# Transposing x and the queries as fp16 pairs read as fp32, with the two head pairs of the query exponentials interleaved

## The chip, the core and the metric

The kernel runs on one core of a Trainium2 chip. The metric is the time of one execution in microseconds (us) on the device; the time of a kernel is the median over its runs. The profile of one execution gives, for every instruction, its engine, its start and its duration. The engines are PE (TensorE, matrix multiplications and transposes; its weight loads are listed apart as PEld), DVE (VectorE), ACT (ScalarE), POOL (GpSimd) and SP (SyncE, which here only issues DMAs).

## What is computed

The input q, k and v have the shape (8 batches, 8 heads, 576 rows, 64 columns). The first part is a linear attention, the second a highway layer on its output, seen as 4608 tokens of 512 columns:

```python
q_s = softmax(q, axis=-1)          # over the 64 columns of a row
k_s = softmax(k, axis=2)           # over the 576 rows of a head
kv = einsum('bhsd,bhse->bhde', k_s, v)
x = einsum('bhsd,bhde->bhse', q_s, kv)   # then (B, S, H*D) -> 4608 x 512
H = maximum(x @ w_h, 0)
T = 1 / (1 + exp(-(x @ w_t + b_t)))
out = T * H + (1 - T) * x
```

All inputs and the output are float32. The softmax of the reference subtracts the maximum first; the kernel takes the exponentials directly and divides by their sums later.

## The kernel before

**Tiles.** The eight batches are taken in pairs. Each pair gives nine tiles of 128 tokens: four from the one batch, four from the other, and one with the 64 last rows of each (`tiles`, lines 125 to 129), so 36 tiles, numbered 0 to 35.

**Steps and their order.** The work is cut into small steps, each a function that records the instructions of one step on one engine. The string `ORDER` (lines 16 to 62), written out in full, names all steps in one sequence. `eq_3_0:F` is the step `eq` with the numbers 3 and 0 and the variant F; a letter A, D or P mostly chooses the engine (ACT, DVE, POOL). Every engine does its steps strictly in the order of this string, and waits where a step needs a result or a free buffer. All loads and nearly all stores are issued by SP, whose queue is in the same order; so a load behind a store waits until that store is ready.

**Per batch b.** `k`, `v` and `q` load float32 tiles with three buffers each. `ek` (L253) takes the exponentials of k on ACT to fp16. `vc` (L259) copies v to fp16. `kv` (L269) multiplies them on PE with 64x64 tiles, `kr` and `kn` (L281, L287) divide by the sums on DVE and write the result `kvb`, block-diagonal over a pair of heads. `eq` takes the exponentials of q on ACT to fp16 (L298, L302, L307). The tile `qe` is then [128 partitions, 9 row groups j, 4 head groups c, 64 columns]; partitions hold two halves of the heads or of the rows, by the batch. `qt` transposes it on PE in pieces of 128x128 fp16 (L319, L324), `qc` (L333) copies the transposed queries from PSUM to the SBUF tile `eq`. Batch 7 is different: its main part is transposed by two DMAs (`qd`, L340), and only its last 64 rows on PE. `WIDE` are batches 4 to 7, whose q is loaded in another layout, `TURNED` is batch 7. The batches 0 and 1 take `eq` in three groups of row groups (`GROUPS`), batch 2 in two halves of head groups, batch 3 and 4 at once (F), the later ones in two halves and a remainder.

**Per tile i.** `xu` (L361) multiplies the transposed queries with `kvb` on PE and gives the unnormalised x with the sums. `rs` and `x` (L370, L376) divide on DVE and write x as fp16. `xt` (L384) transposes x on PE: four transposes of 128x128, each taking every second column of 256 (the rows of w_h and w_t are loaded in the same order, partition p of a block holding rows 2p and 2p+1). They go to the first half of the one PSUM tile `turned`. `xe` (L391) copies it to SBUF as `xT`, on DVE or ACT. `mt` (L411) and `mh` (L419) multiply xT with w_t and w_h, four multiplications of 512 columns each. `bw` (L399) writes the bias into the PSUM tile of the gate first. `th` takes a tanh (L433, L435), `dd` (L439) forms the maximum, `uu` multiplies gate and difference on DVE (L453) or, for 17 tiles, on POOL in two steps (L450, L451), and `oo` (L471) adds x on POOL. `st` stores. Tiles 0, 4 and 5 are done in two halves by head pairs (`HALVED`).

**The start.** `fill` (L167) are dummy multiplications of zeros on PE; they stand between the first steps until about 17 us.

Two identity matrices are built on POOL at the start, `idf` in fp32 and `idh` in fp16; PE's transposes use `idh` as the moving operand and the data as the weights.

Of the kernel before, what the change touches and what calls it, by code (L numbers as in the profile page):

```python
# [8 lines left out]
FP32 = mybir.dt.float32  # L9
FP16 = mybir.dt.float16  # L10
AF = mybir.ActivationFunctionType
# [54 lines left out]
def kernel(  # L66
# [10 lines left out]
    nc = tc.nc  # L77
    B, H, S, D = q.shape
    DM = H * D
    P = 128  # L80
    NP = 64
    NJ = S // NP
# [7 lines left out]
    qep = pool("qep", 2)  # L90
    eqp = pool("eqp", 4)
    xp = pool("xp", 6)
    xtp = pool("xtp", 3)
# [10 lines left out]
    idf = consts.tile([P, P], FP32, name="idf")  # L104
    idh = consts.tile([P, P], FP16, name="idh")
    w16 = {w: consts.tile([P, KC, DM], FP16, name="w16" + w) for w in "th"}
# [8 lines left out]
    turned = ps_xt.tile([P, 2, 4, P], FP16, tag="xtps", name="turned")  # L115
    spare = turned.rearrange("p a c d -> p (a c d)").bitcast(FP32)
    T = {}

    def once(name, make):
        if name not in T:  # L120
            T[name] = make()
        return T[name]
# [10 lines left out]
    def heads(i, k):  # L133
        return (k, k + 1) if i in HALVED else (0, 2)
# [6 lines left out]
    def columns(i, h):  # L141
        return slice(PIECES[h], PIECES[h + 1]) if i == LAST else slice(0, DM)

    def gate(i, h):
        return f"tps{i}_{h}" if i == LAST else f"tps{i}"
# [28 lines left out]
    def landing(which, b):  # L174
        return once(f"{which}32{b}", lambda: ld.tile([P, 4, NJ * D], FP32, tag=which, name=f"{which}32_{b}"))
# [4 lines left out]
    def load_kv(which):  # L180
        def step(e, b, c):
            n = (2 if which == "k" else 1, 2)[b] if b < 2 else 4
            nc.sync.dma_start(landing(which, b)[:, c:c + n], rows_of(which, b)[:, c:c + n])
        return step

    WIDE = (4, 5, 6, 7)
    MAIN = 4 * 2 * 4 * D
    TURNED = (7,)

    def flat_q(b):  # L190
        return landing("q", b).rearrange("p c f -> p (c f)")
# [99 lines left out]

    GROUPS = ((0, 4), (4, 8), (8, 9))

    def eq(e, b, g):
        t = once(f"qe{b}", lambda: qep.tile([P, NJ, 4, D], FP16, tag="qe", name=f"qe_{b}"))
        if b in WIDE:
            if g == 2:
                nc.scalar.activation(t[:, 8], flat_q(b)[:, MAIN:].rearrange("p (c d) -> p c d", c=4), AF.Exp)  # L298
                return
            half = slice(0, 8) if e == "F" else slice(4 * g, 4 * g + 4)  # L300
            src = flat_q(b)[:, 0:MAIN].rearrange("p (c t d) -> p c t d", c=4, t=8)[:, :, half]
            nc.scalar.activation(t[:, half].rearrange("p t c d -> p c t d"), src, AF.Exp)  # L302
            return
        js, cs = slice(*GROUPS[g]), slice(0, 4)
        if b >= 2:
            js, cs = slice(0, NJ), slice(0, 4) if e == "F" else slice(2 * g, 2 * g + 2)
        nc.scalar.activation(t[:, js, cs].rearrange("p j c d -> p c j d"),  # L307
                             T[f"q32{b}"].rearrange("p c (j d) -> p c j d", j=NJ)[:, cs, js], AF.Exp)

    def qt(e, b, g):  # L310
        j0, j1 = GROUPS[g]
        a, s = (2, 2) if g < 2 else (1, 1)
        t = T[f"qps{b}_{g}"] = ps_q.tile([P, a, 4, s * NP], FP16, tag="qps", name=f"qps_{b}_{g}")
        if b in WIDE and g < 2:
            main = T[f"qe{b}"].rearrange("p j c d -> p (j c d)")[:, 0:MAIN]
            main = main.rearrange("p (hh j kk f) -> p j hh kk f", j=4, hh=2, kk=2)
            for jp in (2 * g, 2 * g + 1):
                for n in range(4):
                    nc.tensor.matmul(t[:, jp % 2, n], main[:, jp, n % 2, n // 2], idh,  # L319
                                     is_transpose=True, start=True, stop=True, skip_group_check=True)  # L320
            return
        for j in range(j0, j1):
            for kk in range(2):
                nc.tensor.matmul(  # L324
                    t[:, (j - j0) % 2, 2 * kk:2 * kk + 2].rearrange("p n (t s u) -> p n t s u", s=s, u=2)[:, :, :, (j - j0) // 2],
                    T[f"qe{b}"][:, j, 2 * kk:2 * kk + 2].rearrange("p c d -> p (c d)"), idh,
                    is_transpose=True, start=True, stop=True, skip_group_check=True)

    def qc(e, b, g):
        copy = nc.scalar.copy if e == "A" else nc.vector.tensor_copy  # L330
# [6 lines left out]
    def qd(e, b, g):  # L337
        t = T[f"eq{b}_{g}"] = eqp.tile([P, 2, 4, P], FP16, tag="eq", name=f"eq_{b}_{g}")
        half = MAIN // 2
        nc.sync.dma_start_transpose(t.rearrange("p a n t -> p (a n) t"),  # L340
                                    T[f"qe{b}"].rearrange("p j c d -> p (j c d)")[:, g * half:(g + 1) * half])

    def turned_q(b, jp, n):
        if b in TURNED and jp < 4:
            return T[f"eq{b}_{n % 2}"].rearrange("p a n t -> p (a n) t")[:, 2 * jp + n // 2]
        return T[f"eq{b}_{jp // 2}"][:, jp % 2, n]

    def xu(e, i, k):
        bs, jp = tiles[i]
        k0, k1 = heads(i, k)  # L350
        if i in HALVED:
            t = ps_g.tile([P, DM], FP32, tag="gps", name=f"xu_{i}_{k}").unsqueeze(1)
        else:
            t = ps_x.tile([P, 2, DM], FP32, tag="xu", name=f"xu_{i}")
        T[f"xu{i}_{k}"] = t
        for n in range(2 * k0, 2 * k1):
            kk, hh = n // 2, n % 2
            for w, b in enumerate(bs):
                rows = slice(0, P) if len(bs) == 1 else slice(64 * w, 64 * w + 64)
                dst = t[rows, kk - k0, 0:260].rearrange("p (s e) -> p s e", s=4)[:, hh:hh + 3:2]  # L360
                nc.tensor.matmul(dst, turned_q(b, jp, n), kvb[b % NKV][:, hh, kk],  # L361
                                 start=True, stop=True, skip_group_check=True)
# [15 lines left out]

    def xt(e, i, k):
        k0, k1 = heads(i, k)  # L380
        t = T[f"xtps{i}"] = turned[:, 0]
        for n in range(2 * k0, 2 * k1):
            n0 = n // 2 * 2 * P
            nc.tensor.matmul(t[:, n], T[f"x{i}"][:, n0 + n % 2:n0 + 2 * P:2], idh, is_transpose=True,  # L384
                             start=True, stop=True, skip_group_check=True)

    def xe(e, i, k):
        k0, k1 = heads(i, k)
        t = once(f"xT{i}", lambda: xtp.tile([P, 4, P], FP16, tag="xT", name=f"xT_{i}"))
        copy = nc.vector.tensor_copy if e == "D" else nc.scalar.copy  # L390
        copy(t[:, 2 * k0:2 * k1], T[f"xtps{i}"][:, 2 * k0:2 * k1])  # L391


    def bw(e, i, h=0):
# [8 lines left out]
    def parts_of(i, k):  # L403
        return range(2 * k, 2 * k + 2) if i in HALVED else range(4)

    def mt(e, i, k):
        cs = columns(i, k)
        parts = parts_of(i, k)
        first = once(f"mt{i}", lambda: k) == k and len(parts) < 4
        for n in parts:  # L410
            nc.tensor.matmul(T[gate(i, k)][:, cs], T[f"xT{i}"][:, n], w16["t"][:, n, cs], start=False,  # L411
                             stop=(n == parts[-1] and not first), skip_group_check=True)

    def mh(e, i, k):
        first = f"gps{i}" not in T
        t = once(f"gps{i}", lambda: ps_g.tile([P, DM], FP32, tag="gps", name=f"gps_{i}"))
        parts = parts_of(i, k)
        for n in parts:
            nc.tensor.matmul(t, T[f"xT{i}"][:, n], w16["h"][:, n], start=(first and n == parts[0]),  # L419
                             stop=(n == parts[-1] and not (first and len(parts) < 4)), skip_group_check=True)  # L420


# [50 lines left out]
    def st(e, i, h):  # L473
# [21 lines left out]
        setuppool=setup_pool, setupdve=setup_dve, bsplit=bsplit, fill=fill,  # L495
        k=load_kv("k"), v=load_kv("v"), q=load_q, w=load_w, b=load_b, bp=bp, bc=bc,
        wtc=wt_cast, whc=wh_cast, whd=wh_less_identity, ek=ek, vc=vc, kv=kv, kr=kr, kn=kn, eq=eq, qt=qt, qc=qc, qd=qd,
        xu=xu, rs=rs, x=x, xt=xt, xe=xe, bw=bw, mt=mt, mh=mh, th=th, dd=dd, uu=uu, oo=oo, st=st)
    with tc.manual_schedule():
        for step in ORDER.split():  # L500
            name, _, eng = step.partition(":")
# [32 lines left out]
```

## Time and profile before

| | |
|---|---|
| time, median of 3 runs | 118.87 us (118.81 to 119.09) |
| span of the profiled execution | 116.9 us (no other time of this execution is given) |
| mean granted clock of TensorE | 0.995 |
| busy: PE, PEld | 109.5 us (94%), 61.6 us (53%) |
| busy: DVE, ACT, POOL | 93.3 us (80%), 90.0 us (77%), 89.1 us (76%) |
| DMA | 40.58 MB, mean 347 GB/s |
| x transposes (L384) | 144 of 128x128 fp16 |
| query transposes (L324, L319) | 80 and 48 of 128x128 fp16 |
| multiplications with w_t, w_h (L411, L419) | 148 and 144 |

How to read the rows of the profile: a row of a group gives line, engine, operation, target and sources by the program's names, shapes, the count, then the busy time in us and the mean of one instruction in ns, then the engine's idle time in front of these and what ended it. A row of waits reads "who waited, for whom: us in total, how many times, the longest". A row of the timeline or of the chain begins with the start in us and a duration in us. Matmuls are pipelined: the duration of one contains a latency that overlaps with the next, so that the distance of starts in a series, and not the mean of one, is what an instruction costs. Shares of busy time are means over the whole run; what a change is worth is read at the stage in which it lies.

### The profile page before, as it was taken

To read this page: it belongs to the slowest core of one execution; us is meant where nothing else is said; L and a number is where in the kernel's file an instruction comes from. 1 tells how busy PE (TensorE), PEld (TensorE's weight loads), DVE (VectorE), ACT (ScalarE), POOL (GpSimd) and SP (SyncE) were. 2 spreads that over 40 slices of the span, in tenths; PEclk is the share of its full clock that TensorE was granted. 3 is DMA by queue.
4 is the path that set the end of the run, shared out by engine and by line. 5 is a ranking of instruction groups with operands and counts; after the bars stand their busy time and mean duration, and the time that the engine had idled before them with its cause. 6 is when DMAs were issued, how large, how long until landed. Compare 5 with 4: busy or idle time off the path is not lost.

```text
span 116.9 us, 3424 instructions
## 1 busy us (share of the span) xinstructions
PE 109.5 (94%) x1351; PEld 61.6 (53%) x1351; DVE 93.3 (80%) x222; ACT 90.0 (77%) x132; POOL 89.1 (76%) x99
## 2 busy tenths in 40 slices
PE   5999987999999999999999999999999999999930
PEld 2354544545665656565665547566564555554520
DVE  5642587589799979979889798988989887899870
ACT  4356461897999999989999999998597998545520
POOL 5022237208996999999999999999989699999960
PEclk9999999999999999999999999999999999999998
DMA  2999999999999999999999999999999956992875
GB/s 42 399 392 377 408 398 385 375 377 379 393 391 397 383 391 393 358 375 387 357 376 360 387 392 363 390 381 383 399 398 217 302 204 270 397 404 115 315 295 179
DMA packets 24195, 40.58 MB, mean 347 GB/s; under 512 B 5362, under 2 KB 11762, under 8 KB 24180
## 3 DMA queue, kind: packets, MB, share of 16 engines
q1 hardware_dynamic: 24032, 40.24, 96.9%
q8 instruction: 10, 0.16, 0.6%
q10 hardware_dynamic: 148, 0.14, 0.4%
q14 instruction: 5, 0.04, 0.1%
HBM read 30.41 MB, written 9.44 MB: 341 GB/s over the span
## 4 chain that ended last, share of the span: by engine, by line
PE 67%; POOL 15%; issue 6%; DVE 5%; DMA 3%; SPq 1%; POOLq 0%; DVEq 0%
PE tps L411 18%; PE gps L419 16%; PE turned L167 9%; POOL o L471 7%; PE xu L361 6%; PE turned L384 5%; PE kv L269 5%; PE qps L324 4%; POOL u L451 4%; DMA out_dram<-o 3%; POOL g L450 2%; PE qps L319 2%; POOL v L259 2%; DVE x L376 2%; PE tps L401 1%
## 5 line engine op out<-in xcount | busy, mean ns | idle before, releaser
L471 POOL TENSOR_TENSOR o<-u,x 128x512 f32<-128x512 f16 (+1 forms) x36 | 40.6, 1143 | 1.6 <-DVE u L453 0.7
L411 PE MATMUL tps<-w16t,xT 128*128 128x512 f16 (+1 forms) x148 | 37.3, 373 | 0.0
L419 PE MATMUL gps<-w16h,xT 128*128 128x512 f16 x144 | 36.8, 379 | 0.5 <-DVE xT L391 0.5
L376 DVE TENSOR_TENSOR x<-xu,rs 128x512 f16<-128x512 f32 (+1 forms) x39 | 25.2, 649 | 2.4
L259 POOL CAST v<-v 128x1152 f16<-128x1152 f32 (+1 forms) x14 | 14.0, 1010 | 14.7 <-DMA v<-in_v_dram 13.7
L439 DVE SCALAR_TENSOR_TENSOR d<-x,gps 128x512 f16<-128x512 f16 x36 | 24.5, 680 | 0.3
L451 POOL TENSOR_TENSOR u<-g,d 128x512 f16<-128x512 f16 x17 | 19.7, 1158 | 1.7 <-DVE rs L370 0.4
L253 ACT ACTIVATE ek<-k 128x576 f16<-128x576 f32 (+2 forms) x15 | 17.9, 1225 | 3.0 <-DMA k<-in_k_dram 3.0
L419 PEld LDWEIGHTS <-xT 128*128 128x128 f16 x144 | 13.0, 98 | 12.3 <-DVE xT L391 1.8
L399 ACT COPY tps<-ball 128x512 f32<-128x512 f32 x28 | 16.6, 597 | 3.5 <-DVE u L453 3.2
L411 PEld LDWEIGHTS <-xT 128*128 128x128 f16 x148 | 13.2, 98 | 10.6 <-DVE xT L391 0.4
L361 PE MATMUL xu<-kvb,eq 128*128 128x130 f16 (+1 forms) x160 | 14.8, 224 | 0.2 <-DVE kvb L287 0.2
L384 PE MATMUL turned<-idh,x 128*128 128x128 f16 x144 | 14.2, 220 | 0.5 <-DVE x L376 0.5
L391 DVE COPY xT<-turned 128x512 f16<-128x512 f16 (+1 forms) x28 | 10.9, 391 | 4.2 <-PE turned L384 3.0
L435 ACT ACTIVATE tps<-tps 128x512 f32<-128x512 f32 (+1 forms) x20 | 11.2, 559 | 3.6 <-PE tps L411 3.3
L453 DVE SCALAR_TENSOR_TENSOR u<-tps,d 128x512 f16<-128x512 f32 (+1 forms) x19 | 12.7, 671 | 1.4 <-ACT tps L435 0.6
L361 PEld LDWEIGHTS <-eq 128*128 128x128 f16 (+1 forms) x160 | 10.0, 100 | 7.3 <-DVE x L376 2.5
L167 PE MATMUL turned<-blank 128*128 128x512 f16 x40 | 12.4, 458 | 1.5 <-POOL blank L149 1.3
L384 PEld LDWEIGHTS <-x 128*128 128x128 f16 x144 | 9.8, 98 | 6.0 <-DVE x L376 2.1
L307 ACT ACTIVATE qe<-q 128x1024 f16<-128x1024 f32 (+3 forms) x9 | 9.4, 1052 | 4.1 <-DMA q<-in_q_dram 4.1
L450 POOL TENSOR_SCALAR g<-th 128x512 f16<-128x512 f16 x17 | 10.6, 621 | 0.9 <-ACT th L433 0.9
L433 ACT ACTIVATE th<-tps 128x512 f16<-128x512 f32 x17 | 10.0, 594 | 0.9 <-PE tps L411 0.9
(48 smaller groups left out, 106.8 us busy)
## 6 DMA issues: line engine op xcount, KB each, us to landing
k<-in_k_dram SPq DMA_DIRECT2D x6, 1152.0 KB, 12.2
v<-in_v_dram SPq DMA_DIRECT2D x6, 1152.0 KB, 12.0
out_dram<-o SPq DMA_DIRECT2D x23, 256.0 KB, 4.0
q<-in_q_dram SPq DMA_DIRECT2D x10, 512.0 KB, 11.5
out_dram<-o SPq DMA_DIRECT2D x6, 512.0 KB, 3.8
k<-in_k_dram SPq DMA_DIRECT2D x4, 576.0 KB, 9.3
q<-in_q_dram SPq DMA_DIRECT2D x2, 1152.0 KB, 14.2
q<-in_q_dram SPq DMA_DIRECT2D x2, 640.0 KB, 10.5
```

Source lines behind the costliest of these rows:

```text
L167: nc.tensor.matmul(spare, blank[:, 0:P], blank, start=True, stop=True, skip_group_check=True)
L253: nc.scalar.activation(t[:, :, c:c + n].rearrange("p j c d -> p c j d"), T[f"k32{b}"][:, c:c + n].rearrange("p c (j d) -> p c j d", j=NJ), ...
L259: copy(v16[b % NV][:, c:c + n, :, 0:D], T[f"v32{b}"][:, c:c + n].rearrange("p c (j d) -> p c j d", j=NJ))
L361: nc.tensor.matmul(dst, turned_q(b, jp, n), kvb[b % NKV][:, hh, kk], start=True, stop=True, skip_group_check=True)
L376: nc.vector.tensor_mul(t[:, k0:k1], sums(i, k)[:, :, :, 0:64], T[f"rs{i}_{k}"][:, 0:k1 - k0].unsqueeze(3).to_broadcast([P, k1 - k0, 4, D]))
L384: nc.tensor.matmul(t[:, n], T[f"x{i}"][:, n0 + n % 2:n0 + 2 * P:2], idh, is_transpose=True, start=True, stop=True, skip_group_check=True)
L399: nc.scalar.copy(t[:, cs], ball[:, cs])
L411: nc.tensor.matmul(T[gate(i, k)][:, cs], T[f"xT{i}"][:, n], w16["t"][:, n, cs], start=False, stop=(n == parts[-1] and not first), skip_gro ...
L419: nc.tensor.matmul(t, T[f"xT{i}"][:, n], w16["h"][:, n], start=(first and n == parts[0]), stop=(n == parts[-1] and not (first and len(part ...
L439: nc.vector.scalar_tensor_tensor(t, T[f"x{i}"], -0.5, T[f"gps{i}"], op0=ALU.mult, op1=ALU.max)
L451: nc.gpsimd.tensor_mul(t, g, T[f"d{i}"])
L471: eng.tensor_add(t[:, cs], T[f"u{i}_{h}"][:, cs], T[f"x{i}"][:, cs])
```

## The change

Two fp16 elements that lie side by side are read as one fp32 element, and transposed together. A 128x128 transpose of such pairs moves 128 fp32 columns; the result holds, for each pair, the transposed two elements side by side.

- `xt`: in place of four fp16 transposes with `idh` a tile takes two fp32 ones with `idf`. The tile `xT` has the two elements of a pair innermost; `mt` and `mh` pick one of them with a step of two (`turned_x`).
- `qt`: for a row group j in place of two fp16 transposes there is one fp32 transpose, in the batches 0 to 6, and for the remainder of batch 7. `turned_q` picks with a step of two.
- `eq`: in order that the right elements be neighbours, the two head pairs (k = 0, 1) are interleaved element by element when the exponentials are written. One instruction writes one head pair, to every second fp16 element. For batches 0 and 1 in each of the two main groups, and for batches 3 and 4 (F), there are then two instructions where there was one. Batches 2, 5 and 6 had two already: their halves are now the head pairs (5 and 6 had halves of the row groups). The remainders (g = 2) stay one instruction. Batch 7's main part is written as before and still transposed by DMA.

ORDER, all pools, loads and stores stay as they are. The core of the diff (the unchanged lines around and the DMA step's renaming are cut):

```diff
     def eq(e, b, g):
...
+        exp = lambda dst, src: nc.scalar.activation(dst, src, AF.Exp)
+        pairs = flat_qe(b).rearrange("p (j w d k) -> p k w j d", j=NJ, w=2, k=2)
+        if b in WIDE and g == 2:
+            exp(pairs[:, :, :, 8], flat_q(b)[:, MAIN:].rearrange("p (k w d) -> p k w d", k=2, w=2))
+            return
+        if b in TURNED:
...
+        ks, js = (0, 1), slice(0, 8) if b in WIDE else slice(0, NJ)
+        if b >= 2:
+            ks = (0, 1) if e == "F" else (g,)
+        else:
+            js = slice(*GROUPS[g])
...
+        if b < 2 and g == 2:
+            exp(pairs[:, :, :, 8], src[:, :, :, 8])
+            return
+        for k in ks:
+            exp(pairs[:, k, :, js], src[:, k, :, js])
 
     def qt(e, b, g):
...
+        q32 = flat_qe(b).bitcast(FP32).rearrange("p (j f) -> p j f", j=NJ)
...
+        t32 = t.rearrange("p a n t -> p (a n t)").bitcast(FP32).rearrange("p (a h t) -> p a h t", a=a, h=2)
+        turn = lambda dst, src: nc.tensor.matmul(dst, src, idf, is_transpose=True, start=True, stop=True,
+                                                 skip_group_check=True)
         if b in WIDE and g < 2:
...
             for jp in (2 * g, 2 * g + 1):
-                for n in range(4):
-                    nc.tensor.matmul(t[:, jp % 2, n], main[:, jp, n % 2, n // 2], idh,
-                                     is_transpose=True, start=True, stop=True, skip_group_check=True)
+                for hh in range(2):
+                    turn(t32[:, jp % 2, hh], q32[:, 4 * hh + jp])
             return
         for j in range(j0, j1):
-            for kk in range(2):
-                nc.tensor.matmul(
...
+            turn(t32[:, (j - j0) % 2].rearrange("p h (t s u) -> p h t s u", s=s, u=2)[:, :, :, (j - j0) // 2], q32[:, j])
 
     def turned_q(b, jp, n):
...
-        return T[f"eq{b}_{jp // 2}"][:, jp % 2, n]
+        t = T[f"eq{b}_{jp // 2}"][:, jp % 2].rearrange("p n t -> p (n t)").rearrange("p (h t k) -> p h t k", h=2, k=2)
+        return t[:, n % 2, :, n // 2]
 
     def xt(e, i, k):
         k0, k1 = heads(i, k)
-        t = T[f"xtps{i}"] = turned[:, 0]
-        for n in range(2 * k0, 2 * k1):
-            n0 = n // 2 * 2 * P
-            nc.tensor.matmul(t[:, n], T[f"x{i}"][:, n0 + n % 2:n0 + 2 * P:2], idh, is_transpose=True,
+        T[f"xtps{i}"] = turned[:, 0].rearrange("p n t -> p (n t)").rearrange("p (c t r) -> p c t r", c=2, r=2)
+        pairs, turned_pairs = T[f"x{i}"].bitcast(FP32), spare[:, 0:2 * P].rearrange("p (c t) -> p c t", c=2)
+        for c in range(k0, k1):
+            nc.tensor.matmul(turned_pairs[:, c], pairs[:, c * P:(c + 1) * P], idf, is_transpose=True,
                              start=True, stop=True, skip_group_check=True)
 
+    def turned_x(i, n):
+        return T[f"xT{i}"][:, n // 2, :, n % 2]
...
-            nc.tensor.matmul(T[gate(i, k)][:, cs], T[f"xT{i}"][:, n], w16["t"][:, n, cs], start=False,
+            nc.tensor.matmul(T[gate(i, k)][:, cs], turned_x(i, n), w16["t"][:, n, cs], start=False,
...
-            nc.tensor.matmul(t, T[f"xT{i}"][:, n], w16["h"][:, n], start=(first and n == parts[0]),
+            nc.tensor.matmul(t, turned_x(i, n), w16["h"][:, n], start=(first and n == parts[0]),
```

More of the change, by code (lines that the diff above doesn't have):

```diff
@@ L292, with flat_qe @@
     GROUPS = ((0, 4), (4, 8), (8, 9))
+    def flat_qe(b):
+        return once(f"qe{b}", lambda: qep.tile([P, NJ * 4 * D], FP16, tag="qe", name=f"qe_{b}"))
     def eq(e, b, g):
-        t = once(f"qe{b}", lambda: qep.tile([P, NJ, 4, D], FP16, tag="qe", name=f"qe_{b}"))
-        if b in WIDE:
[L297 to L302, printed above, removed]
-            return
[L304 to L308, printed above, removed]
+        exp = lambda dst, src: nc.scalar.activation(dst, src, AF.Exp)
[4 more added lines that the diff above has]
+        if b in TURNED:
+            src = flat_q(b)[:, 0:MAIN].rearrange("p (c t d) -> p t c d", c=4, t=8)[:, 4 * g:4 * g + 4]
+            exp(flat_qe(b)[:, 0:MAIN].rearrange("p (t c d) -> p t c d", t=8, c=4)[:, 4 * g:4 * g + 4], src)
+            return
[4 more added lines that the diff above has]
+            js = slice(*GROUPS[g])
+        if b in WIDE:
+            src = flat_q(b)[:, 0:MAIN].rearrange("p (k w j d) -> p k w j d", k=2, w=2, j=8)
+        else:
+            src = T[f"q32{b}"].rearrange("p (k w) (j d) -> p k w j d", k=2, j=NJ)
+        if b < 2 and g == 2:
+            exp(pairs[:, :, :, 8], src[:, :, :, 8])
+            return
+        for k in ks:
+            exp(pairs[:, k, :, js], src[:, k, :, js])
     def qt(e, b, g):
@@ L312, in qt @@
         a, s = (2, 2) if g < 2 else (1, 1)
+        q32 = flat_qe(b).bitcast(FP32).rearrange("p (j f) -> p j f", j=NJ)
         t = T[f"qps{b}_{g}"] = ps_q.tile([P, a, 4, s * NP], FP16, tag="qps", name=f"qps_{b}_{g}")
+        t32 = t.rearrange("p a n t -> p (a n t)").bitcast(FP32).rearrange("p (a h t) -> p a h t", a=a, h=2)
+        turn = lambda dst, src: nc.tensor.matmul(dst, src, idf, is_transpose=True, start=True, stop=True,
+                                                 skip_group_check=True)
         if b in WIDE and g < 2:
-            main = T[f"qe{b}"].rearrange("p j c d -> p (j c d)")[:, 0:MAIN]
-            main = main.rearrange("p (hh j kk f) -> p j hh kk f", j=4, hh=2, kk=2)
             for jp in (2 * g, 2 * g + 1):
-                for n in range(4):
-                    nc.tensor.matmul(t[:, jp % 2, n], main[:, jp, n % 2, n // 2], idh,
-                                     is_transpose=True, start=True, stop=True, skip_group_check=True)
+                for hh in range(2):
+                    turn(t32[:, jp % 2, hh], q32[:, 4 * hh + jp])
             return
         for j in range(j0, j1):
-            for kk in range(2):
[L324 to L327, printed above, removed]
+            turn(t32[:, (j - j0) % 2].rearrange("p h (t s u) -> p h t s u", s=s, u=2)[:, :, :, (j - j0) // 2], q32[:, j])
     def qc(e, b, g):
@@ L340, in qd @@
         nc.sync.dma_start_transpose(t.rearrange("p a n t -> p (a n) t"),
-                                    T[f"qe{b}"].rearrange("p j c d -> p (j c d)")[:, g * half:(g + 1) * half])
+                                    flat_qe(b)[:, g * half:(g + 1) * half])
     def turned_q(b, jp, n):
@@ L388, in xe @@
         k0, k1 = heads(i, k)
-        t = once(f"xT{i}", lambda: xtp.tile([P, 4, P], FP16, tag="xT", name=f"xT_{i}"))
+        t = once(f"xT{i}", lambda: xtp.tile([P, 2, P, 2], FP16, tag="xT", name=f"xT_{i}"))
         copy = nc.vector.tensor_copy if e == "D" else nc.scalar.copy
-        copy(t[:, 2 * k0:2 * k1], T[f"xtps{i}"][:, 2 * k0:2 * k1])
+        copy(t[:, k0:k1].rearrange("p c t r -> p (c t r)"),
+             T[f"xtps{i}"][:, k0:k1].rearrange("p c t r -> p (c t r)"))
+    def turned_x(i, n):
+        return T[f"xT{i}"][:, n // 2, :, n % 2]
     def bw(e, i, h=0):
```

## The prediction

> **What bounds the kernel now.** I read the page's strip of 40 slices first, then busy time by stretch, the chain that ended last, and the waits of POOL. The strip (tenths busy per slice of 2.9 us) shows that from slice 8 on nothing has room:
>
> ```profile
> PE   5999987999999999999999999999999999999930
> DVE  5642587589799979979889798988989887899870
> ACT  4356461897999999989999999998597998545520
> POOL 5022237208996999999999999999989699999960
> DMA  2999999999999999999999999999999956992875
> ```
>
> PE runs from slice 7 on without a hole; POOL is full from about 27 us, ACT from about 26 to 82 us, and the DMA engines from 3 to 87 us. Busy PE can be a slow PE, so the chain matters more (start, us, engine, line):
>
> ```profile
> 70.69 0.45 PE qps L319 x8
> ...
> 73.03 0.86 PE gps L419 x4
> ...
> 75.97 0.22 PE turned L384 x4
> ```
>
> Between 20 and 83 us the chain is made of PE steps that follow each other at exactly such lengths. Eight query transposes take 0.45 us, 56 ns each; four x transposes 0.22 us; four multiplications of 512 columns 0.86 us, 215 ns each. So on PE the number of moving columns sets the time. The weight loads lie under it, though one alone is longer than a transpose:
>
> ```profile
> L411 PEld LDWEIGHTS <-xT 128*128 128x128 f16 x148 | 13.2, 98 | 10.6 <-DVE xT L391 0.4
> L384 PEld LDWEIGHTS <-x 128*128 128x128 f16 x144 | 9.8, 98 | 6.0 <-DVE x L376 2.1
> ```
>
> The second row is also the answer to an edit below: L384 already loads every second fp16 column of x, at 98 ns, the same as the contiguous load of L411.
>
> From 83 us on the chain runs through POOL. POOL's work from 27 us on is a queue in fixed order, and it hardly waits (its other five groups of waits all end by 26.56 us and are left out):
>
> ```profile
> POOL v L259 <- PE tps L411: 0.9, 1, 0.9
> POOL g L450 <- ACT th L433: 0.9, 1, 0.9
> POOL o L471 <- DVE u L453: 0.7, 2, 0.5
> POOL u L451 <- DVE rs L370: 0.4, 1, 0.4
> ```
>
> ```profile
> 26.56 0.67 POOL L259 CAST v<-v 128x576 f16<-128x576 f32 x1 [3.86 <-DMA v<-in_v_dram]
> ...
> 111.61 1.82 POOL L471 TENSOR_TENSOR o<-u,x 128x512 f32<-128x512 f16 x2 [0.49 <-DVE u L453]
> ```
>
> Its stretch begins at 26.56, released by a load and not by PE, and ends at 113.43. All its waits inside add to 0.9 + 0.9 + 0.7 + 0.4 = 2.9 us. The change takes no work from POOL, so **2.9 us is the most that any saving on PE can give**.
>
> **The profiled execution.** Its span is 116.9 us; the median of the runs shown is 118.87, 1.97 more. I take those 1.97 us as outside the span and unchanged, and state times against the median.
>
> **The change on PE.** Every pair of fp16 transposes becomes one transpose of the same 128 moving columns, with elements of four bytes. Where they stand, in the stretch in which PE has no hole (us, busy and count of PE, then of the loads):
>
> ```profile
> 20.00:112.00 92.00, 13.42 (x136) 9.30 (x136) 1.00 1.01 356
> 20.00:112.00 92.00, 5.63 (x62) 3.98 (x62) 1.00 1.01 356
> 20.00:112.00 92.00, 3.67 (x48) 3.03 (x48) 1.00 1.01 356
> ```
>
> These are x (L384), and the queries (L324, L319): 246 transposes, which become 123. The 26 before 20 us lie among dummy multiplications and waits and I cost them at nothing; their cover is the fill work (L167). No fp32 matmul or load stands in this trace. The bounds: the cheapest is the row of equal column count, 56 ns, so a pair goes from 112 to 56 and PE loses 123 x 56 ns = 6.9 us. The dearest is the row of four times the columns, 215 ns (four passes): PE gains 123 x (215 - 112) = 12.7 us. Even is 112 ns. I take 56, or up to about 100 if the weight load of 98 ns shows: it is nearest in kind, the same operation with the same number of columns, and columns are what set every PE row above.
>
> The Trainium skill, "TensorE: Matmul & The Clock Gate", section Terms, says of the transpose mode that loads and multiplications got on trn2 that it makes FP32 four times faster; by that a pair costs one pass and PE saves the 6.9 us. No run so far shows it.
>
> **The other edits on PE.** The multiplications by w_t, w_h and the xu products now load every second column of xT and eq: 98 ns by the L384 row above, against 98, so nothing. The copies out of PSUM (L391, L333) move the same flat fp16 elements: nothing. DMA bytes, the queue order of SP and POOL, and batch 7's two DMA transposes are untouched.
>
> **The change on ACT.** The query exponentials are split by head pair where one instruction covered both: eq_0_0, eq_0_1, eq_1_0, eq_1_1, eq_3 and eq_4, six instructions more. The fixed cost of one, from two lengths:
>
> ```profile
> L307 ACT ACTIVATE qe<-q 128x1024 f16<-128x1024 f32 x4 | 4.2, 1058 | 4.1 <-DMA q<-in_q_dram 4.1
> L307 ACT ACTIVATE qe<-q 128x2304 f16<-128x2304 f32 x1 | 2.1, 2127 | 0.0
> L253 ACT ACTIVATE ek<-k 128x2304 f16<-128x2304 f32 x5 | 10.6, 2122 | 0.0
> L302 ACT ACTIVATE qe<-q 128x2048 f16<-128x2048 f32 x1 | 1.9, 1919 | 0.0
> ```
>
> (2127 - 1058) / 1280 = 0.835 ns per element, and 1058 - 1024 x 0.835 = 203 ns fixed: 1.2 us in all. Of the first four, three are done before PE comes to their turn; behind eq_1_0 the turn waits,
>
> ```profile
> PEld L324 <- ACT qe L307: 0.6, 1, 0.6
> ```
>
> so 0.2 us of it reach PE; eq_3 and eq_4 add 0.4 to a full ACT (41 and 53 us), of which ACT's own waits on PE take back some. I charge 0.5 us. Writing at a step of two fp16 elements is in no row; lower bound nothing (it writes the same count), upper bound double the 0.835 ns for 7 x 2304 elements, 13.5 us. I take nothing: L253 and L302, with other layouts of source and target, fit the same rate (203 + 2048 x 0.835 = 1913, measured 1919).
>
> **What of 6.9 us can reach the end.** A faster PE meets the loads. The last k tile is issued, lands (a window that holds this issue alone), is exponentiated, and then used for kv on PE:
>
> ```profile
> 77.69 0.59 SPq L183 DMA_DIRECT2D k<-in_k_dram  x1
> ```
>
> ```profile
> DMA to landing us min/median/max: 11.5/11.5/11.5
> ```
>
> ```profile
> 90.11 2.12 ACT L253 ACTIVATE ek<-k 128x2304 f16<-128x2304 f32 x1
> ```
>
> ```profile
> 92.80 0.78 PE L269 MATMUL kv<-v,ek 64*64 64x65 f16 x72
> 93.51 0.40 PE L384 MATMUL turned<-idh,x 128*128 128x128 f16 x4
> ...
> 108.88 0.39 PE L384 MATMUL turned<-idh,x 128*128 128x128 f16 x4
> ```
>
> It lands at 77.69 + 11.5 = 89.2, with the DMA engines full until 87 us by the strip; the earliest end of its exponential is 91.3, so this kv step (92.80) can move by about 1.4 us and no more, though PE has saved 107 x 56 ns = 6.0 us by then. Behind it stand seven x turns (the first and last shown) and two short q turns, 16 pairs: 16 x 56 = 0.9 us. Together 2.3 us, under POOL's 2.9. Less 0.5 for ACT: 1.8, and 0.1 for handovers that do not close up: a gain of 1.7 us, **117.2 us** (span 115.2). This hardly depends on the exact price: with each weight load after a group's first exposed, two x turns take 98 + 56 = 154 instead of 222 ns and four q turns 350 instead of 448; by 92.8 us that is 27 x 68 + 13 x 98 ns = 3.1 us, still more than 1.4, the tail gives 0.5, and the end gains about 1.3: 117.6.
>
> **Rivals.**
>
> *Four passes.* An fp32 matrix multiplication split into passes would cost 215 ns per turn, by the 512-column row. PE is full from 20 to 112 us, so 12.7 us go straight to the end, with 0.5 of ACT: 132 us. It decides from 112 ns up. Against it: nothing in the profile; for it: nothing either. The Trainium skill, "FP8 and Floating Point Precision", TensorE Precision Notes, says that true FP32 takes four passes through the array; that is a statement on products, and gives the 132 us if turns are treated alike. Chance 0.15.
>
> *The weight load no longer hides (the other side of my forecast).* Today 98 ns of load lie under 56 ns turns, so two loads overlap. If a four-byte load cannot run under the turn before it, each fp32 turn costs 98 + 56 = 154 ns, 42 more than the pair it replaces; 123 x 42 = 5.2 us, on a PE without holes: 118.87 + 5.2 + 0.5 = 124.5. It decides from 56 ns of exposed load per turn. For it: in the profile a load is longer than a turn; against: 512 columns ahead of a first turn hide a load. The Trainium skill, "TensorE: Matmul & The Clock Gate", section Weight-path perf modes, says that the fast weight load is off for FP32 input, and the section LDWEIGHTS gives columns / 1.2 ns: an estimate of 107 ns, 163 ns per turn and 125.6 us by it. Chance 0.13.
>
> *Hidden anyway.* If POOL's waits and the k_7 landing do not move at all, because loads queue behind stores that POOL paces, the saving ends as PE idle and ACT's 0.5 us cancel the 0.9 of the tail: 118.5, within 0.3% of 118.87 to slightly faster. Chance 0.08.
>
> *ACT becomes the bound.* PE saves, but strided exponentials run slower by half, 6.7 us more on an ACT that is full between 26 and 82 us and idles only 1 to 2 us in it; some 2 to 5 us reach the end: 121 to 124. It decides from about 20% more per element. Against: the single rate above. Chance 0.07.
>
> **How the numbers follow.** Forecast 0.57 (117.2, own range 116.2 to 118.3), hidden 0.08, ACT 0.07, exposed load 0.13, four passes 0.15. Below 116.2 (POOL's 2.9 us nearly all gained) I leave 0.04; the four-pass time at 132 is left out above; so 116.2 to 125.6 holds 0.81. Against the 0.3% that a measurement tells here (0.36 us): faster is the forecast but for 0.04 of it that lands short, and a little of "hidden", 0.55; same 0.07; slower 0.38, the last three rivals and some loss by the order of work.
>
> **What would show it.** Right: two fp32 turns of x per tile at about 0.11 us together in the chain, and half as many query turns; POOL waits under 2.9 us in sum; PE with holes that wait for DVE x or xT; ek of batch 7 waiting for its k load near 89 us; ACT 1.2 us busier. Wrong: two turns that take 0.3 or 0.43 us, PE full and everything else with gaps; interleaved exponentials of 1152 elements longer than 1.2 us; or POOL's first o later than 27.2 us.

## The result, and the profile after

The changed kernel takes 120.31 us (120.22 to 120.87), the kernel before, run beside it, 118.93: a ratio of 1.0131, 95% interval 1.0108 to 1.0154. It is slower by about 1.4 us (difference of the medians) to 1.6 us (by the ratio), where 117.2 us was forecast. The span of the profiled execution is 118.6 us against 116.9.

First the turns (a turn is one transpose on PE). This is PE's timeline of the changed kernel (start, duration, line, operation, count):

```profile
45.43 0.39 PE L394 MATMUL turned<-idf,x 128*128 128x128 f32 x2
45.65 0.60 PE L328 MATMUL qps<-idf,qe 128*128 128x128 f32 x4
46.09 1.03 PE L425 MATMUL tps<-w16t,xT 128*128 128x512 f16 x4
...
85.56 0.43 PE L371 MATMUL xu<-kvb,eq 128*64 128x130 f16 x8
85.92 0.44 PE L394 MATMUL turned<-idf,x 128*128 128x128 f32 x2
86.19 1.03 PE L425 MATMUL tps<-w16t,xT 128*128 128x512 f16 x4
```

From start to start, two fp32 turns take 45.65 - 45.43 = 0.22 us, four 0.44: 0.11 us each, as much as the two fp16 turns that each replaces. PE saved nothing. In the last group, behind a step with 64-wide weights, the pair takes 0.27; the same group of the kernel before takes 0.24:

```profile
84.07 0.43 PE L361 MATMUL xu<-kvb,eq 128*64 128x130 f16 x8
84.43 0.40 PE L384 MATMUL turned<-idh,x 128*128 128x128 f16 x4
84.67 1.03 PE L411 MATMUL tps<-w16t,xT 128*128 128x512 f16 x4
```

The weight loads became longer, and the interleaved exponentials too (groups by shape of the changed kernel; the last two numbers before the second bar are busy us and the mean in ns):

```profile
L394 PEld LDWEIGHTS turned<-idf,x 128*128 128x128 f32 x72 | 8.6, 141 | 5.9 <-DVE x L386 1.8 <-ACT xT L401 0.9 <-DVE xT L401 0.2
L298 ACT ACTIVATE qe<-q 128x1024 f16<-128x1024 f32 x8 | 10.3, 1300 | 0.0
L298 ACT ACTIVATE qe<-q 128x1152 f16<-128x1152 f32 x4 | 5.8, 1500 | 0.0
L298 ACT ACTIVATE qe<-q 128x512 f16<-128x512 f32 x8 | 5.6, 763 | 4.5 <-DMA q<-in_q_dram 4.5
L401 DVE COPY xT<-turned 128x512 f16<-128x512 f16 x23 | 9.5, 413 | 2.9 <-PE turned L394 2.3 <-ACT qe L298 0.4
```

(1500 - 763) / 640 = 1.15 ns per element, where the contiguous exponentials had 0.835. (Two of the eight exponentials of 1024 elements are batch 7's, which are still written contiguously; their group is a mixture.) ACT's busy time on the page:

```profile
PE 110.0 (93%) x1215; PEld 61.6 (52%) x1215; DVE 93.8 (79%) x222; ACT 94.0 (79%) x138; POOL 89.1 (75%) x99
```

It is 94.0 us, against 90.0; POOL's is unchanged. PE now waits for the exponentials at more places; before, its loads waited 0.6 us once:

```profile
PEld qps L328 <- ACT qe L298: 2.6, 5, 0.8
PE qps L328 <- ACT qe L298: 0.7, 2, 0.5
```

The first row is of the weight loads, whose waits lie partly under running products; in the second PE itself stands still.

One such place is on the chain, which now leaves PE between 49 and 56 us:

```profile
48.43 0.88 PE gps L433 x4
49.31 0.05 issue
49.36 0.63 ACT th L447
...
53.91 2.57 ACT qe L298 x2
56.48 0.04 issue
56.52 0.66 PE qps L328 x4
```

Batch 4's exponentials ran from 53.15 to 55.07 and its turn began at 55.45 in the kernel before:

```profile
53.15 1.92 ACT L302 ACTIVATE qe<-q 128x2048 f16<-128x2048 f32 x1
```

```profile
55.45 0.61 PE L319 MATMUL qps<-idh,qe 128*128 128x128 f16 x8
```

Now they end at 56.48 and PE turns at 56.52, 1.07 us later. Not all of this arises here: the exponentials already began 0.76 us later (53.91 against 53.15), and took 0.65 us longer. The products with w_t and w_h, 292 in the same order in both traces, let one follow the delay. These are two pairs of the chains, first before, then after:

```profile
47.83 0.86 PE gps L419 x4
48.43 0.88 PE gps L433 x4
...
81.01 0.86 PE gps L419 x4
82.50 0.86 PE gps L433 x4
```

The changed kernel is 0.60 us behind at the first pair, 1.49 at the second and 1.65 at the last product. So the delay builds up in steps before, at and after batch 4's exponentials.

### The profile page after: what moved, and what is told of

Its sections match the earlier page's. It is cut to its first block, busy times and chain, and to the rows that moved or that the text cites. A ratio compares the mean times of both kernels' runs of the same rounds, so it can differ in the third digit from the quotient of the medians.

```text
span 118.6 us, 3165 instructions
## 1 busy us (share of the span) xinstructions
PE 110.0 (93%) x1215; PEld 61.6 (52%) x1215; DVE 93.8 (79%) x222; ACT 94.0 (79%) x138; POOL 89.1 (75%) x99
## 4 chain that ended last, share of the span: by engine, by line
PE 53%; DMA 19%; POOL 9%; ACT 7%; SPq 4%; issue 3%; DVE 1%; POOLq 0%
PE tps L425 17%; PE gps L433 16%; DMA q<-in_q_dram 11%; DMA v<-in_v_dram 6%; PE qps L328 6%; PE xu L371 5%; POOL o L485 5%; PE turned L394 5%; PE kv L269 4%; ACT qe L298 3%; POOL u L465 3%; DMA out_dram<-o 3%; SPq L183 2%; POOL g L464 2%; ACT xT L401 1%
## 5 line engine op out<-in xcount | busy, mean ns | idle before, releaser
L298 ACT ACTIVATE qe<-q 128x512 f16<-128x512 f32 (+3 forms) x26 | 24.4, 979 | 4.5 <-DMA q<-in_q_dram 4.5
L433 PEld LDWEIGHTS <-xT 128*128 128x128 f16 x144 | 13.5, 98 | 12.6 <-DVE xT L401 1.7
L425 PEld LDWEIGHTS <-xT 128*128 128x128 f16 x148 | 14.1, 99 | 10.6 <-DVE xT L401 0.3
L394 PE MATMUL turned<-idf,x 128*128 128x128 f32 x72 | 14.6, 282 | 0.5 <-DVE x L386 0.5
L371 PEld LDWEIGHTS <-eq 128*128 128x128 f16 (+1 forms) x160 | 10.7, 101 | 7.7 <-DVE x L386 2.8
L167 PE MATMUL turned<-blank 128*128 128x512 f16 x40 | 11.1, 420 | 1.5 <-POOL blank L149 1.3
L328 PE MATMUL qps<-idf,qe 128*128 128x128 f32 x64 | 11.3, 283 | 0.9 <-ACT qe L298 0.7
L464 POOL TENSOR_SCALAR g<-th 128x512 f16<-128x512 f16 x17 | 10.5, 620 | 1.4 <-ACT th L447 1.2
L394 PEld LDWEIGHTS turned<-idf,x 128*128 128x128 f32 x72 | 8.6, 141 | 5.9 <-DVE x L386 1.8
```

What stands on the lines that cost most here:

```text
L298: exp = lambda dst, src: nc.scalar.activation(dst, src, AF.Exp)
L328: turn = lambda dst, src: nc.tensor.matmul(dst, src, idf, is_transpose=True, start=True, stop=True, skip_group_check=True)
L394: nc.tensor.matmul(turned_pairs[:, c], pairs[:, c * P:(c + 1) * P], idf, is_transpose=True, start=True, stop=True, skip_group_check=True)
L425: nc.tensor.matmul(T[gate(i, k)][:, cs], turned_x(i, n), w16["t"][:, n, cs], start=False, stop=(n == parts[-1] and not first), skip_group_ ...
L433: nc.tensor.matmul(t, turned_x(i, n), w16["h"][:, n], start=(first and n == parts[0]), stop=(n == parts[-1] and not (first and len(parts) ...
```

## The experiments

Two theories about the loss. **A**: the loss is ACT's; the fp32 turns are neutral on PE. **B**: the loss is PE's, by longer weight loads and by reads of every second column. Ratios are to the kernel before, with 95% intervals.

### x alone

```diff
 # kernel before, with the changed xt, xe, mt, mh only
```

> Only x is turned as fp32 pairs; queries and exponentials as before. Theory A (the loss is ACT's: interleaved writes run at 1.15 instead of 0.835 ns per element, while one fp32 turn costs PE the 0.11 us of the two fp16 turns it replaces): no change, 118.9 us within 0.3. Theory B (the loss is PE's: the fp32 weight loads of 141 instead of 98 ns, and the loads of every second column of xT, delay it): about half of the 1.4 us, 119.4 to 120.

119.32 us, ratio 1.0026 (1.0006 to 1.0045). Between the theories: not the half of B, but not nothing.

### Queries alone

```diff
 # changed kernel, with the xt, xe, mt, mh of before
```

> Only the queries are turned as pairs, with the interleaved exponentials; x as before. Theory A: the whole loss, 120.3 us within 0.3. Theory B: the other half, 119.4 to 119.9.

120.37 us, ratio 1.0114 (1.0082 to 1.0146). Nearly all of the loss comes with the queries, of which this run has both the interleaved exponentials and the fp32 turns.

### The interleaved exponentials alone

```diff
 # kernel before, with the changed eq; qt turns fp16, from every second column
+    q16[:, 4 * (n % 2) + jp, n // 2:4 * D:2], idh
```

> Exponentials written interleaved, as in the changed kernel, but turned by two fp16 transposes that load every second column; x as before; no fp32 turn anywhere. Theory A: the whole loss, 120.3 us within 0.3. Theory B: as before, 118.9.

119.99 us, ratio 1.0073 (1.0044 to 1.0103), without any fp32 turn. ACT is busy for 93.7 us, and its group of 1152 elements shows the same price:

```profile
L298 ACT ACTIVATE qe<-q 128x1152 f16<-128x1152 f32 x4 | 5.9, 1508 | 0.0
```

### The fp32 turns alone

```diff
 # changed kernel, with the eq of before
+    t = flat_qe(b).rearrange("p (j c d) -> p j c d", j=NJ, c=4)
```

> The changed kernel with x and queries turned as fp32 pairs, but the query exponentials written as in the kernel before (contiguous, unsplit); so the paired elements are neighbouring columns of one head and not those of two head pairs, and the products use the wrong ones: a kernel for the time only. Theory A: 118.9 us within 0.3. Theory B: 120.3.

119.57 us, ratio 1.0038 (1.0017 to 1.0059). This is neither of the two. Of the 1.31% of the whole change 0.73% come with the interleaving alone and 0.38% with the turns alone; the 0.20% that are left lie within the intervals. So A explains somewhat more than half, and neither theory is the whole.

### The splits without the interleaving

```diff
+            for cs in (slice(0, 2), slice(2, 4)) if e == "F" else (slice(0, 4),):
+                nc.scalar.activation(t[:, half, cs]..., src[:, cs, half], AF.Exp)
```

> The kernel before with the six query exponentials split in two by head pair, as in the change, but written contiguously and turned by fp16 transposes. Prediction's term: 1.2 us more on ACT, 0.5 us at the end, 119.4. If the write rate alone makes the loss of the interleaved exponentials (0.9 us): 118.9. If the splits make it all: 119.8.

119.04 us, ratio 1.0006 (0.9992 to 1.0021): no difference. ACT's busy time rises by 0.4 us only:

```profile
PE 109.2 (93%) x1351; PEld 61.7 (53%) x1351; DVE 93.3 (80%) x222; ACT 90.4 (77%) x138; POOL 88.9 (76%) x99
```

The mean of one instruction contains a part that overlaps with its neighbour: in this run an exponential of 512 elements that takes 0.63 us is followed by the next 0.54 us after its start. So six instructions more do not cost six times the 203 ns. Of the 4.0 us in the changed kernel, 0.4 go with the splits, and the 3.6 that remain are put down to the slower elements.

### Interleaved by the reads and not by the writes

```diff
-        pairs = ... "p (j w d k) -> p k w j d"      # one head pair k at a time, step of two
+        pairs = ... "p (j w d k) -> p w j d k"      # one w at a time, k innermost: whole runs
```

> The changed kernel, but each query exponential now covers one half of every head pair's partner (one w) and both head pairs, so that ACT writes runs of 128 neighbouring fp16 elements and instead reads alternately from two distant float32 places; same number of instructions. If the write at a step of two elements is what costs 1.15 ns per element, this one returns to 0.835 (1152 elements: 1.16 us instead of 1.50) and the time falls to that of the pairs with plain exponentials plus the splits, 119.6 to 119.9 us. If any interleaving costs it, 1.50 us and 120.3.

120.10 us, ratio 1.0104 (1.0082 to 1.0126), neither of the two:

```profile
L298 ACT ACTIVATE qe<-q 128x1152 f16<-128x1152 f32 x4 | 5.6, 1413 | 0.0
L298 ACT ACTIVATE qe<-q 128x512 f16<-128x512 f32 x8 | 5.5, 735 | 4.4 <-DMA q<-in_q_dram 4.2
```

(1413 - 735) / 640 = 1.06 ns per element. Whole runs on the writing side, with reads that jump between two places, are nearly as dear as whole reads with stepped writes. So it is not the write alone; what the two have in common is not settled.

### Where ACT's time reaches the end

```diff
+        if b not in (3, 4):
+            return eq_plain(e, b, g)
```

> All turns as fp32 pairs, but the exponentials interleaved and split only for batches 3 and 4 and plain for all others (whose products then use the wrong pairs: for the time only). Between all plain (119.57) and all interleaved (120.31) lie 0.74 us. If the delay arises where the chain of the changed kernel runs through ACT (49 to 56 us, ending in batch 4's exponentials), these two batches make most of it: 120.1 to 120.3. If each batch adds its share (2 of 7): 119.8.

119.95 us, ratio 1.0074 (1.0053 to 1.0094): 0.38 of the 0.74 us by the medians, 0.36 of 0.93% by the ratios to the kernel before beside each; so four to five tenths, and not "most". That is more than two batches' proportional share (119.8), but within the uncertainty of both numbers.

The traces say more. This is how much each kernel falls further behind the kernel before in three stretches (times of the kernel before), by the starts of the same products with w_t and w_h (one execution each; three runs without a slowdown, the splits, the stepped reads and POOL's relief, stay within 0.13 us in each stretch):

| delay added (us) | 23 to 47 us | 47 to 58 us | 58 us to the end |
|---|---|---|---|
| changed kernel | 0.43 | 0.56 | 0.48 |
| this run (fp32 turns, 3 and 4 interleaved) | 0.13 | 0.55 | 0.36 |
| fp32 turns, plain exponentials | 0.11 | 0.16 | 0.46 |
| interleaved exponentials, fp16 turns | 0.45 | 0.41 | 0.18 |

Batches 3 and 4 make the middle column, and the batches before them the first. In the last column the kernels with fp32 turns lose 0.36 to 0.48 us whether or not the later batches are interleaved, so most of that goes with the turns.

### What sets the price of an fp32 turn

```diff
-    matmul(turned_pairs[:, c], pairs[:, c * P:(c + 1) * P], idf, ...)
+    matmul(turned_pairs[:, c, 0:64], pairs[0:64, c * P:(c + 1) * P], idf[0:64, 0:64], ...)   # 64 moving
+    matmul(turned_pairs[0:64, c], pairs[:, c * P:c * P + 64], idf, ...)                      # 64 of weights
```

> The changed kernel with x turned for 64 of 128 tokens only: each fp32 turn moves 64 columns, with weights of 128 columns and 64 rows; the other half of xT keeps old values: for the price of a turn only. If the moving columns set the 0.11 us of a turn, two turns take 0.11 us together; if its weight load does, 0.22 as before.

> The changed kernel with each fp32 turn of x loading 64 instead of 128 columns of weights and moving all 128 columns; the other half of xT keeps old values: for the price of a turn only. The run with half the moving columns took no less per pair (0.26 us), which speaks for the weight load. If the load sets the 0.11 us of a turn, two turns take about 0.11 to 0.15 us together; if the moving fp32 columns do, 0.22 as before.

With 64 moving columns (and 64 rows) a pair took 0.26 us and no less; its weight load and its first turn start together, 43.94 and 43.95, behind the products of 43.60. So the load is exposed, and the run says nothing on the price of a column:

```profile
43.60 0.41 PE L371 MATMUL xu<-kvb,eq 128*128 128x130 f16 x4
43.95 0.34 PE L394 MATMUL turned<-idf,x 64*128 64x64 f32 x2
44.21 1.90 PE L433 MATMUL gps<-w16h,xT 128*128 128x512 f16 x8
```

With half the weights the load falls to 111 ns, and the pair stays at 0.22 us (62.56 - 62.34):

```profile
62.34 0.38 PE L394 MATMUL turned<-idf,x 128*64 128x128 f32 x2
62.56 1.03 PE L433 MATMUL gps<-w16h,xT 128*128 128x512 f16 x4
...
85.69 0.43 PE L371 MATMUL xu<-kvb,eq 128*64 128x130 f16 x8
86.05 0.41 PE L394 MATMUL turned<-idf,x 128*64 128x128 f32 x2
86.29 1.03 PE L425 MATMUL tps<-w16t,xT 128*128 128x512 f16 x4
```

So the expectation that the first of these runs had raised, that the load sets the price, falls. What is left is the 128 fp32 columns themselves, at twice the time of fp16 ones; whether reading them or writing their wider results takes the time, no run separates. Behind the 64-wide step the pair is back at 0.24: the 0.03 us more in the changed kernel there is the longer load. (Times of these two runs, 123.07 and 120.39, are of one execution each.)

### What is left of x alone

```diff
 # x alone as pairs, each turn with 64 of its 128 weight columns
 # and: kernel before, mt and mh load every second column of xT
```

> Only x turned as fp32 pairs, and each turn loads 64 of its 128 weight columns (half of xT keeps old values: for the time only). With x alone as pairs the time rose by 0.26%, and the traces show a full fp32 load at 141 ns that is exposed by about 0.04 us where the step before has 64-wide weights, against 111 ns for this half load. If those exposed loads made the 0.3 us: back to 118.9 within 0.15. If the longer stream of the fp32 turns, or the steps of two in xT, made it: 119.2 to 119.4.

> The kernel before with fp16 turns, but the multiplications with w_t and w_h load every second column of xT, as in the changed kernel (the columns are then not the right ones: for the time only). If the reads at a step of two make the 0.2 to 0.3% that x as pairs costs: 119.2 to 119.4. If they cost nothing, as the prediction had it: 118.9 within 0.15.

Half the load: ratio 1.0021 (1.0003 to 1.0039), not to be told from the 1.0026 with the whole load. Step reads alone: 118.90 us, ratio 1.0000 (0.9984 to 1.0017). The stepped reads are ruled out; how much of the 0.3 us is the exposed load stays open.

### Was there a gain to be had at all?

```diff
-        for n in range(2 * k0, 2 * k1):
+        for n in range(2 * k0, 2 * k1, 4):        # one x transpose of four (kernel before)
```

> The kernel before with only one of four x transposes per tile made (one of two in a half tile); the rest of the turned tile keeps old values, all other work is done: a kernel for the time only. It takes 99 x 56 ns = 5.5 us from PE after 20 us, to test the cap of the prediction, which could not be seen because PE saved nothing. By the prediction's working (1.4 us up to the last kv step, 7 x 168 ns = 1.2 behind it, under POOL's 2.9): 116.3 to 116.7 us. Rival, PE alone is the bound: 113.4. Rival, hidden by the other engines: 118.5 to 118.9.

118.50 us, ratio 0.9964 (0.9948 to 0.9981): of 5.5 us taken from PE 0.4 us reach the end. The chain of this run is made of loads and POOL; here are the two loads of v in its middle and the copies that they release:

```profile
22.95 14.65 DMA v<-in_v_dram
...
37.71 1.14 POOL v L259
...
49.84 12.82 DMA v<-in_v_dram
...
62.78 1.29 POOL v L259 x2
```

In the kernel before, POOL's first copy of these started at 37.64, and the wait of 0.9 us ahead of it was listed under PE. It is a load's: the load landed at 37.52 there too, and with PE relieved the copy did not start earlier. POOL's last work ends at 112.27 instead of 113.43, so 1.2 us were won by then in this execution; but the last stores took longer to land, 3.6 to 3.9 us here,

```profile
DMA to landing us min/median/max: 3.6/3.7/3.9
```

against 2.2 to 2.5 in the kernel before, and the span is 117.1 us against 116.9. Why, no run shows; one more profile, below, has the same.

```diff
-            nc.gpsimd.tensor_scalar(g, T[f"th{i}"], 1.0, 1.0, op0=ALU.add, op1=ALU.mult)
-            nc.gpsimd.tensor_mul(t, g, T[f"d{i}"])
+            nc.gpsimd.tensor_mul(t, T[f"th{i}"], T[f"d{i}"])
```

> The kernel before without the step that adds 1 to the tanh on POOL (L450): 17 x 0.62 = 10.5 us less on POOL, all else as before; the gate lacks the 1: for the time only. Theory C (PE, POOL and the loads bind the kernel before together, so that relieving one gives nearly nothing): 118.5 to 118.9. If POOL alone binds: under 117.

> Both reliefs in the kernel before: POOL without that step, and one x transpose of four (5.5 us less on PE); for the time only. PE alone relieved gave 118.5. If POOL held it there, this one falls well below, to 116 to 117.3 us (the 2.3 us that the last k load leaves by the prediction's working). If the loads hold it: 118.2 to 118.5.

10.5 us less on POOL alone: 119.01 us, ratio 1.0005 (0.9983 to 1.0026). Both reliefs: 118.20 us, ratio 0.9934 (0.9912 to 0.9957). The time is as expected if the loads hold it. The chain runs through the load of batch 6's k until 73 us, then through ACT and DVE to 87 us, and through PE behind:

```profile
61.37 11.98 DMA k<-in_k_dram
73.35 0.02 issue
73.38 0.92 ACT ek L253
```

That load lands no earlier than in the kernel before (72.80), and the last k load at 89.46, against 89.21. At the end it is again the stores: POOL is done at 112.08, 1.35 us earlier than before, and the last three stores take

```profile
DMA to landing us min/median/max: 3.3/3.5/3.7
```

so that the span is 116.7 us. Loads that land no earlier and stores that land later both keep the saving from the end; how much each does in the median, these two profiles don't tell.

## Why the prediction was wrong

- **"I take 56"** for an fp32 turn: this is the step that failed. It is 111 ns, between the bounds of 56 and 215 and at the "even is 112" of the text. The row taken as nearest had the same number of columns, but no row had a moving element wider than fp16; the lower bound was chosen by kinship alone. With 111 the saving of 6.9 us is nothing, and the dearer load and the slower exponentials are left. The Trainium skill, "TensorE: Matmul & The Clock Gate", section Terms, calls the transpose mode four times faster for FP32, but does not say than what; no run here has another fp32 multiplication to compare with. Measured, an fp32 turn costs twice an fp16 one.
- **Stepped reads of weights and the copies out of PSUM at nothing**: right (1.0000 in the run with only the reads; the copy 413 ns before and after).
- **"I take nothing" for the stepped write**: wrong, and the larger part of the loss: 1.15 instead of 0.835 ns, some 3.6 us of ACT. The bound of 13.5 us was there; the reason given against it, that contiguous rows fit one rate, said nothing on a layout that none of them had. The Trainium skill, "ScalarE: Activation LUTs", section What ACT_TABLE_LOAD costs, gives one element per cycle at 1.2 GHz whatever the function; the contiguous rows agree (0.835 ns), the interleaved ones do not (1.15 and 1.06).
- **0.5 us for the splits**: too much; alone they make no measurable difference (1.0006), and ACT's busy time rises by 0.4 us and not by 1.2.
- **"What of 6.9 us can reach the end"**: the direction was right, most of it is hidden, but 2.3 us was far too much: 0.4 of 5.5 came through. In the profiled execution the engines did end 1.2 us earlier, and the last stores took that back, of which the working had no term. POOL's wait of 0.9 us listed under PE was a load's, and I had counted it as PE's; the loads of v in the middle, just in time, were not looked at, only the last k.
- **The rivals.** Four passes: no, 111 and not 215 ns. The load that no longer hides: not 98 ns for each turn; a first load shows by 0.03 to 0.04 us in places. ACT becomes the bound: this is the one that came nearest. Its threshold, 20% per element, was passed (38%), but its price of 2 to 5 us was, even at its lower end, more than twice too high: with the interleaving alone ACT is busy for 3.7 us more (93.7 us) and the time rises by 0.9. ACT had more room than the text said: from 26 to 82 us it is busy for 53.31 us of 56, so 2.7 us were idle and not 1 to 2; in the changed kernel it is 55.02. The run that took 5.5 us from PE ended at 118.50, the time that "Hidden anyway" gives; so that rival stood nearer than its chance of 0.08 said.

## What to carry to other kernels

Pairing 16-bit elements does not make a PE transpose cheaper here; before restructuring for it, measure one fp32 turn in place of two fp16 ones. Price the producer's new layout too: an engine with little room passes on a part of every slower element (here 0.9 of 3.7 us), and a rate seen on contiguous rows says nothing on an interleaved one. And where PE, POOL, ACT and the loads are all full, relieve one of them in a throwaway kernel first: it shows in one run whether any saving there can reach the end.

## What the runs showed that was not expected

- An fp32 turn streams its 128 columns in 111 ns, twice the fp16 time, with 128 as with 64 columns of weights; its full load takes 141 ns against 98.
- ACT's exponential takes 1.15 ns per element when it writes every second fp16 element, and 1.06 when it writes whole runs but reads alternately from two places, against 0.835.
- With PE relieved, POOL ended 1.2 and 1.35 us earlier in the two profiled executions, but the last stores took 3.3 to 3.9 us to land instead of 2.2 to 2.5; the cause is open.
- Removing 10.5 us from POOL, busy from 27 us to the end, changed the time by 0.05% (within the interval).
